# Chunks 4 to 7 score eight heads at once in two banks, and all later scores leave out the masked quarter

## The chip, the core and the metric

The kernel runs on one core of a Trainium2 chip. Its engines work from queues of their own: TensorE (PE, with its weight loads as PEld), VectorE (DVE), ScalarE (ACT), GpSimdE (POOL) and SyncE (SP, which issues most of the DMAs). The metric is the device time of one execution in microseconds (us), as the median of several runs; lower is better.

## What is computed

Three stages follow each other; the text is cut to what matters here. q, k and v have 4 batches, 8 heads, 768 positions and 64 columns a head.

```python
# retention, position by position
state = gamma * state + k[t]^T v[t]                     # 64 x 64 for each batch and head
y[t]  = 0.125 * q[t] state
x = y as 3072 tokens x 512
xn = x / sqrt(mean(x*x) + 1e-6) * rms_g                 # gated layer
x = (silu(xn @ w_gate) * (xn @ w_val)) @ w_out          # 512 -> 1536 -> 512
h = x @ w_in                                            # 512 -> 1024
solu = h * softmax(h);  ln = layernorm(solu) * g_ln
out = ln @ w_out2                                       # 1024 -> 512
```

The retention is computed in chunks of 128 positions. Within a chunk, key j and query i give a score k_j . q_i, which is multiplied by 0.125 gamma^(i-j) for i >= j and by 0 for i < j (the table `mtab`); the product, called A, is multiplied by v. What came before the chunk enters through the state U.

## The kernel before

**Blocks and chunks.** The 3072 tokens are 6 blocks of 512, and a block is 4 chunks of 128: chunks 4 to 7 belong to block 1, chunks 8 to 11 to block 2, and so on; a batch is six chunks. Block n's two layers run on PE while the chunks of block n+1 are worked on between their matmuls. So chunks 4 to 7 are computed during block 0 (from about 35 to 156 us), the others during blocks 1 to 4.

**The layers.** Each block has 12 steps m. A step is 12 matmuls for the gate into bank GB, 12 for the values into VB and 12 for the output of the step before into the four X banks; a product is three matmuls (L687 to L689: high x high, high x low, low x high), each of 512 columns in a 32-bit format. ACT makes silu from GB (L732), DVE multiplies it with VB (L704).

**The weights in block 0.** They come as 64-bit integers and are converted in 36 pieces (piece g, part 0 to 2, for step g), each some steps before PE needs it. The chain of one piece: a DMA on SP into one of four buffers `x` (L563), ACT L585, DVE L587, POOL L588, then ACT takes the signs of the piece into the PSUM bank YB (`conv_g`, L593) and DVE multiplies by them (`conv_b`, L600). ACT makes the high part (L91), DVE or POOL the low part (L92), into `w`, `wo` or `CV`, and ACT's queue stores both. In block 0 the bank YB serves the signs alone, one piece after another.

**Chunks 4 to 7 (units).** A unit is four heads of a chunk; u = 0 or 1. `unit_scores` (L159) makes four matmuls over 64 rows into bank SB, 128 x 128 each, one after another since all four lie in the same half of the rows; DVE masks them (L161). `unit_out` computes the output and the new state for the four heads, and loads what the unit after the next needs. `unit_prep` makes the decayed k and q on POOL (L143, L151).

**Chunks 8 to 23.** `att_scores` (L110 as the line of the helper) makes eight heads: the even heads lie in rows 0 to 63 and go to SB, the odd ones in rows 64 to 127 and go to YB, so two matmuls run beside each other. DVE masks bank by bank (L229). `att_out` follows some slots later; its first matmuls (SB/YB<-qd,U) are 64 x 64 and use all four quarters of the array.

**The order.** The program is written slot by slot (`slot`, `w_slot`); a scheduling layer then orders the instructions of each engine by its own model of their times, and inserts waits. Each engine runs its queue in order, so an instruction that waits holds up what is behind it.

Of the kernel before, what the change touches and what calls it, by code (L numbers as in the profile page):

```python
# [18 lines left out]
P = 128  # L19
# [21 lines left out]
def retention_moe_kernel(ctx: ExitStack, tc: tile.TileContext, qk0, q2, kt, kv, wpk, w2i, w2o,  # L41
# [38 lines left out]

    def st():
        return wt("st", [P, 512], F32, 3)
# [44 lines left out]
    def unit_load(gc, u):  # L127
        tq = wt("rq", [P, 4, P], F32, 2)
        nc.sync.dma_start(tq, q2[gc, u])
        if u == 0:  # L130
            rawk[gc] = wt("rk", [P, 4, P], F32, 2)
            nc.sync.dma_start(rawk[gc], kt[gc])
        tv = wt("rv", [P, 512], F32, 2)
        nc.sync.dma_start(tv, kv[gc, u])
        raw[gc, u] = (tq, tv)

    def unit_prep(gc, u):
        tq, tv = raw.pop((gc, u))
        tk = rawk[gc] if u == 0 else rawk.pop(gc)
        kd = qd = None  # L140
        if gc % CPB != CPB - 1:
            kd = wt("kd", [P, 4, 64], F32, 2)
            nc.gpsimd.tensor_tensor(  # L143
                out=kd, in0=tv[:, 0:256].rearrange("p (h d) -> p h d", h=4),
                in1=ktab_t[:, 4 * u:4 * u + 4].unsqueeze(2).to_broadcast([P, 4, 64]), op=ALU.mult)
        if gc % CPB != 0:
            qd = wt("qd", [P, 2, P], F32, 2)
            tq4 = tq.rearrange("p (a b) i -> p a b i", b=2)
            for hh in range(2):
                r = halfrows(hh)  # L150
                nc.gpsimd.tensor_tensor(out=qd[r], in0=tq4[r, :, hh, :],  # L151
                                        in1=qtab_t[r, 2 * u:2 * u + 2, :], op=ALU.mult)
        r = halfrows(u)
        prepd[gc, u] = (tk[r], tq[r], tv, kd, qd)
# [9 lines left out]
    def unit_out(gc, u):  # L164

        tk, tq, tv, kd, qd = prepd.pop((gc, u))
        A = masked.pop((gc, u))
        first, last = gc % CPB == 0, gc % CPB == CPB - 1
        ps = slice(2 * u, 2 * u + 2)
        calls = []  # L170
        if not first:
            calls += [mm(SB[:, pl * P:pl * P + P], U[gc % 2][:, 2 * u + pl, :], qd[:, pl, :], pl == 0, False)
                      for pl in range(2)]
        for pl in range(2):
            for hh in range(2):
                hl = 2 * pl + hh
                calls.append(mm(SB[halfrows(hh), pl * P:pl * P + P], tv[:, 256 + 64 * hl:320 + 64 * hl],
                                A[:, hl, :], first, first or pl == 1))
        sv = SB[:, 256:384].rearrange("p (a e) -> p a e", a=2)
        if not last:  # L180
            for pl in range(2):
                for hh in range(2):
                    hl = 2 * pl + hh
                    calls.append(mm(sv[halfrows(hh), pl, :], kd[:, hl, :], tv[:, 256 + 64 * hl:320 + 64 * hl],
                                    True, True))
# [12 lines left out]
    def att_load(gc):  # L198
        tq, tk = wt("rq", [P, 4, P], F32, 2), wt("rk", [P, 4, P], F32, 2)
        tv = wt("rv", [P, 2, 512], F32, 2)  # L200
# [5 lines left out]
        nc.sync.dma_start(tv, kv[gc].rearrange("u p x -> p u x"))  # L206
        raw[gc] = (tq, tk, tv)

    def att_prep(gc):
        tq, tk, tv = raw.pop(gc)  # L210
        kd = qd = None
        if gc % CPB != CPB - 1:
            kd = wt("kd", [P, 2, 4, 64], F32, 2)
# [8 lines left out]
    def att_scores(gc):  # L222
        tq, tk = prepd[gc][0:2]
        banks = (SB, YB)
        run([mm(banks[hh][:, p * P:p * P + P], tk[halfrows(hh), p, :], tq[halfrows(hh), p, :], True, True)
             for p in range(4) for hh in (1, 0)])
        for hh in (1, 0):
            A = masked[gc, hh] = wt("A", [P, 4, P], F32, 2)
            nc.vector.tensor_tensor(out=A, in0=banks[hh].rearrange("p (a i) -> p a i", a=4),  # L229
                                    in1=mtab_t[:, hh::2, :], op=ALU.mult)  # L230
# [239 lines left out]
    def att_pieces(n):  # L470

        out = []
        if n == 1:
            units = [(gc, u) for gc in range(NCB, 2 * NCB) for u in range(2)]
            ahead = units + [(2 * NCB,), (2 * NCB + 1,)]
            for i, (gc, u) in enumerate(units):
                nxt, nx2 = ahead[i + 1], ahead[i + 2]

                def a(gc=gc, u=u, nxt=nxt):
                    unit_scores(gc, u)  # L480

                def b(nxt=nxt):
                    (unit_prep if len(nxt) == 2 else att_prep)(*nxt)

                def c(gc=gc, u=u, nx2=nx2):
                    unit_out(gc, u)
                    (unit_load if len(nx2) == 2 else att_load)(*nx2)

                out += [a, b, c]
# [718 lines left out]
```

## Time and profile before

| | |
|---|---|
| runs | 993.92, 994.65 and 995.5 us, median 994.65 |
| profiled execution | 994.05 us, of which its span, first to last instruction, is 992.3 |
| PE busy | 978.1 us, 99% of the span |
| DVE, ACT, POOL busy | 453.7, 397.6 and 412.8 us |
| DMA | 211.59 MB, 213 GB/s as a mean |

Busy times overlap, since the engines run beside each other. In the timeline a row begins with its start and its duration in us, and a PE row's end is modelled: matmuls overlap, so what one costs is read from the distance between starts. One 32-bit matmul of the attention is two records. The note in brackets at a row's end is the idle time of the engine before it and who ended it.

### The profile page before, as it was taken

To read this page: it belongs to the slowest core of one execution; us is meant where nothing else is said; L and a number is where in the kernel's file an instruction comes from. 1 tells how busy PE (TensorE), PEld (TensorE's weight loads), DVE (VectorE), ACT (ScalarE), POOL (GpSimd) and SP (SyncE) were. 2 spreads that over 40 slices of the span, in tenths; PEclk is the share of its full clock that TensorE was granted. 3 is DMA by queue.
4 is the path that set the end of the run, shared out by engine and by line. 5 is a ranking of instruction groups with operands and counts; after the bars stand their busy time and mean duration, and the time that the engine had idled before them with its cause. 6 is when DMAs were issued, how large, how long until landed. Compare 5 with 4: busy or idle time off the path is not lost.

```text
span 992.3 us, 15224 instructions
## 1 busy us (share of the span) xinstructions
PE 978.1 (99%) x5654; PEld 814.7 (82%) x5654; DVE 453.7 (46%) x857; ACT 397.6 (40%) x770; POOL 412.8 (42%) x453
## 2 busy tenths in 40 slices
PE   8999999999999999999999999999999999999998
PEld 7778787888888888888888888888888888999887
DVE  5798784552453633233462223463223353443552
ACT  4767664681353452222453223334212344221433
POOL 6976883770142582252543233644032382000031
PEclk9899999999999999999999999999999999999999
DMA  9699999886412135897523889612597724687200
GB/s 353 242 329 408 351 324 347 319 321 218 164 54 86 44 125 178 292 337 262 163 75 106 287 286 311 224 49 104 174 344 266 265 79 149 216 303 257 75 8 36
DMA packets 90187, 211.59 MB, mean 213 GB/s; under 512 B 9729, under 2 KB 35713, under 8 KB 90113
## 3 DMA queue, kind: packets, MB, share of 16 engines
q1 hardware_dynamic: 81328, 185.45, 54.9%
q10 hardware_dynamic: 8784, 25.17, 6.5%
q8 instruction: 45, 0.74, 0.3%
q14 instruction: 30, 0.24, 0.1%
HBM read 171.78 MB, written 38.80 MB: 212 GB/s over the span
## 4 chain that ended last, share of the span: by engine, by line
PE 91%; POOL 3%; DMA 2%; DVE 1%; issue 1%; ACT 1%; SPq 0%; ACTq 0%; POOLq 0%
PE X L687 12%; PE X L689 12%; PE X L688 12%; PE GB L687 7%; PE GB L689 7%; PE GB L688 7%; PE VB L687 6%; PE VB L688 6%; PE VB L689 6%; PE SB L110 3%; PE YB L110 2%; PE YB L793 2%; PE VB L793 2%; PE SB L793 1%; PE GB L793 1%
## 5 line engine op out<-in xcount | busy, mean ns | idle before, releaser
L704 DVE TENSOR_TENSOR f<-VB,f 128x512 f32<-128x512 f32 x60 | 41.4, 690 | 164.0 <-PE VB L689 156.1
L688 PE MATMUL X<-r,wo 128*128 128x512 f32 x264 | 103.6, 392 | 0.0
L689 PE MATMUL X<-r,wo 128*128 128x512 f32 x264 | 103.0, 390 | 0.0
L687 PE MATMUL X<-r,wo 128*128 128x512 f32 x264 | 101.5, 396 | 0.6 <-DMA wo<-scr 0.6
L732 ACT ACTIVATE f<-GB 128x512 f32<-128x512 f32 x60 | 35.7, 595 | 153.3 <-PE GB L689 147.4
L91 ACT CAST r<-f 128x512 fp32r<-128x512 f32 x72 | 44.6, 620 | 123.6 <-DVE f L704 104.1
L588 POOL TENSOR_TENSOR st<-st,x 128x512 int32<-128x512 int32 x52 | 71.2, 1374 | 47.4 <-DVE st L587 17.0
L687 PE MATMUL GB<-xnh,w 128*128 128x512 f32 (+1 forms) x220 | 86.6, 394 | 0.8 <-ACT xnh L345 0.4
L687 PE MATMUL VB<-xnh,w 128*128 128x512 f32 (+1 forms) x220 | 85.9, 391 | 1.1 <-DVE f L704 1.1
L688 PE MATMUL GB<-xnl,w 128*128 128x512 f32 (+1 forms) x220 | 85.7, 390 | 0.5 <-DVE xnl L92 0.4
L689 PE MATMUL GB<-xnh,w 128*128 128x512 f32 (+1 forms) x220 | 85.6, 389 | 0.0
L689 PE MATMUL VB<-xnh,w 128*128 128x512 f32 (+1 forms) x220 | 85.3, 388 | 0.3 <-POOL w L92 0.3
L688 PE MATMUL VB<-xnl,w 128*128 128x512 f32 (+1 forms) x220 | 85.2, 387 | 0.0
L92 DVE TENSOR_TENSOR r<-f,r 128x512 fp32r<-128x512 f32 x72 | 62.4, 868 | 31.3 <-ACT r L91 30.8
L528 POOL TENSOR_TENSOR x<-x 128x512 f32<-128x512 f32 x24 | 31.1, 1296 | 107.3 <-DMA x<-scr 88.4
L918 POOL TENSOR_TENSOR sm<-sm 128x1 f32<-128x1 f32 x24 | 4.9, 202 | 138.6 <-DVE sm L896 116.4
L687 PEld LDWEIGHTS X<-r,wo 128*128 128x128 f32 x264 | 49.3, 188 | 11.7 <-issue 1.3
L689 PEld LDWEIGHTS X<-r,wo 128*128 128x128 f32 x264 | 49.6, 188 | 10.4
L688 PEld LDWEIGHTS X<-r,wo 128*128 128x128 f32 x264 | 49.7, 188 | 10.0 <-issue 0.2
L687 PE MATMUL X<-w2oh,r 128*128 128x512 f32 (+1 forms) x144 | 56.6, 393 | 0.0
L689 PE MATMUL X<-w2oh,r 128*128 128x512 f32 (+1 forms) x144 | 56.0, 389 | 0.0
L688 PE MATMUL X<-w2ol,r 128*128 128x512 f32 (+1 forms) x144 | 55.4, 385 | 0.0
(369 smaller groups left out, 2411.1 us busy)
## 6 DMA issues: line engine op xcount, KB each, us to landing
w<-scr SPq DMA_DIRECT2D x96, 512.0 KB, 4.8
wo<-scr SPq DMA_DIRECT2D x60, 512.0 KB, 4.5
x<-in_wpk SPq DMA_DIRECT2D x36, 512.0 KB, 6.2
x<-scr SPq DMA_DIRECT2D x24, 512.0 KB, 5.6
sscr<-x SPq DMA_DIRECT2D x24, 512.0 KB, 7.5
scr<-CV ACTq DMA_DIRECT2D x18, 512.0 KB, 6.4
rv<-in_kv SPq DMA_DIRECT2D x16, 512.0 KB, 4.2
scr<-w ACTq DMA_DIRECT2D x12, 512.0 KB, 5.3
```

What stands on the lines that cost most here:

```text
L91: h = nc.scalar.copy(hi, src)
L92: (lo_eng or nc.vector).tensor_tensor(out=lo, in0=src, in1=hi.bitcast(F32), op=ALU.subtract)
L110: return lambda: nc.tensor.matmul(out, lhsT=lhsT, rhs=rhs, start=start, stop=stop)
L528: nc.gpsimd.tensor_tensor(out=w[:, 0, :], in0=w[:, 0, :], in1=w[:, 1, :], op=ALU.add)
L588: nc.gpsimd.tensor_tensor(out=ti, in0=ti, in1=lo, op=ALU.add)
L687: nc.tensor.matmul(ps, lhsT=lh, rhs=rh, start=start, stop=False)
L688: nc.tensor.matmul(ps, lhsT=lh, rhs=rl, start=False, stop=False)
L689: nc.tensor.matmul(ps, lhsT=ll, rhs=rh, start=False, stop=stop)
L704: recent["dve"] = nc.vector.tensor_tensor(out=a, in0=GV[1], in1=silu[:, 0, :], op=ALU.mult)
L732: recent["act"] = nc.scalar.activation(s[:, 0, :], GV[0], AF.Silu)
L793: nc.tensor.matmul(ps, lhsT=x, rhs=y[:, k, :], start=start and k + i == 0, stop=k == 1 and i == 2, skip_group_check=True)
L918: G.tensor_tensor(out=w, in0=r, in1=r, op=ALU.mult)
```

## The change

For chunks 4 to 7 the units are gone. `att_load`, `att_prep` and `att_scores` serve them as they serve the later chunks, and `half_out` computes output and state for four of the eight heads at a time, in SB, with the same matmuls as `unit_out`. Since `att_scores` writes YB too, the signs of the weights (`conv_g`) and the scores use that bank in turns.

In `att_scores` each head is now two matmuls instead of one: keys 0 to 63 against all 128 queries, and keys 64 to 127 against queries 64 to 127. The quarter with late keys and early queries, where the mask is 0, is left out, and POOL sets it to 0 in A. Each matmul fills a quarter of the array (64 rows, 64 columns). For heads 4 to 7 the key halves are swapped in the output rows, so that four neighbours in the program use four different quarters; for that `att_load` loads v with its halves swapped and `turn_tables` loads the halves of `mtab` and `ktab` again the other way round. The mask is three DVE instructions a bank instead of one. `gap` only moves addresses.

```diff
-    def unit_load(gc, u):
...
-    def unit_scores(gc, u):
-        tk, tq, tv, kd, qd = prepd[gc, u]
-        for hl in range(4):
-            nc.tensor.matmul(SB[:, hl * P:hl * P + P], lhsT=tk[:, hl, :], rhs=tq[:, hl, :], start=True, stop=True)
-        A = masked[gc, u] = wt("r2", [P, 4, P], F32, 8)
-        nc.vector.tensor_tensor(out=A, in0=SB.rearrange("p (h i) -> p h i", h=4),
-                                in1=mtab_t[:, 4 * u:4 * u + 4, :], op=ALU.mult)
...
+    def half_out(gc, u):
+        tq, tk, tv, kd, qd = prepd[gc] if u == 0 else prepd.pop(gc)
+        A = [masked[gc, hh] if u == 0 else masked.pop((gc, hh)) for hh in range(2)]
...
     def att_load(gc):
...
-        nc.sync.dma_start(tv, kv[gc].rearrange("u p x -> p u x"))
+        nc.sync.dma_start(tv[:, 0], kv[gc, 0])
+        for r in range(2):
+            nc.sync.dma_start(tv[halfrows(r), 1], kv[gc, 1, halfrows(1 - r)])
+
+    def turn_tables():
+        for r in range(2):
+            nc.sync.dma_start(mtab_t[halfrows(r), 4:8, :], mtab[halfrows(1 - r), 4:8, :])
+            nc.sync.dma_start(ktab_t[halfrows(r), 4:8], ktab[halfrows(1 - r), 4:8])
...
     def att_scores(gc):
...
-        run([mm(banks[hh][:, p * P:p * P + P], tk[halfrows(hh), p, :], tq[halfrows(hh), p, :], True, True)
-             for p in range(4) for hh in (1, 0)])
+        def score(hh, p, jb):
+            half = jb if p < 2 else 1 - jb
+            return mm(banks[hh][halfrows(half), p * P + 64 * jb:p * P + P], tk[halfrows(hh), p, halfrows(jb)],
+                      tq[halfrows(hh), p, 64 * jb:P], True, True)
+
+        run([score(hh, p, jb) for jb in range(2) for a in range(2)
+             for hh, p in ((1, a), (0, 2 + a), (1, 2 + a), (0, a))])
         for hh in (1, 0):
             A = masked[gc, hh] = wt("A", [P, 4, P], F32, 2)
-            nc.vector.tensor_tensor(out=A, in0=banks[hh].rearrange("p (a i) -> p a i", a=4),
-                                    in1=mtab_t[:, hh::2, :], op=ALU.mult)
+            sc, mt = banks[hh].rearrange("p (a i) -> p a i", a=4), mtab_t[:, hh::2, :]
+            early, late = slice(0, 64), slice(64, P)
+            for ps, hs, ts_ in ((slice(0, P), slice(0, 4), late), (halfrows(0), slice(0, 2), early),
+                                (halfrows(1), slice(2, 4), early)):
+                nc.vector.tensor_tensor(out=A[ps, hs, ts_], in0=sc[ps, hs, ts_], in1=mt[ps, hs, ts_], op=ALU.mult)
+            for ps, hs in ((halfrows(0), slice(2, 4)), (halfrows(1), slice(0, 2))):
+                nc.gpsimd.memset(A[ps, hs, early], 0.0)
...
         if n == 1:
-            units = [(gc, u) for gc in range(NCB, 2 * NCB) for u in range(2)]
...
+            for gc in range(NCB, 2 * NCB):
+                out += [lambda gc=gc: att_scores(gc), lambda gc=gc: att_prep(gc + 1), lambda gc=gc: half_out(gc, 0),
+                        lambda gc=gc: (half_out(gc, 1), att_load(gc + 2))]
             return out
...
-    unit_load(NCB, 0)
-    unit_load(NCB, 1)
-    unit_prep(NCB, 0)
+    turn_tables()
+    att_load(NCB)
+    att_load(NCB + 1)
+    att_prep(NCB)
```

What the scheduling layer makes of it is shown at three places. The first is DVE's queue while PE works on step 4 of block 0. Before, a unit's mask (L161) stands between the sign products (L600, which read YB) and concerns SB only:

```order
L587 TENSOR_SCALAR st_858<-x_96_811 128x512
L600 SCALAR_TENSOR_TENSOR st_830<-st_830,YB 128x512
L161 TENSOR_TENSOR r_111_922<-SB,mtab_t 128x512
L92 TENSOR_TENSOR CV<-st_830,CV 128x512
L587 TENSOR_SCALAR st_899<-x_99_835 128x512
```

The same place in the changed kernel, where L582 is the sign product, L569 the first shift of a piece, L223 the mask and L686 the product with VB:

```order
L582 SCALAR_TENSOR_TENSOR st_810<-st_810,YB 128x512
L99 TENSOR_TENSOR r_103_939<-f_98_910,r_102_938 128x512
L99 TENSOR_TENSOR wo_886<-st_810,wo_886 128x512
L569 TENSOR_SCALAR st_891<-x_87_815 128x512
L223 TENSOR_TENSOR A_874<-YB,mtab_t 128x4x64
L223 TENSOR_TENSOR A_874<-YB,mtab_t 64x2x64 x2
L223 TENSOR_TENSOR A_880<-SB,mtab_t 128x4x64
L223 TENSOR_TENSOR A_880<-SB,mtab_t 64x2x64 x2
L582 SCALAR_TENSOR_TENSOR st_839<-st_839,YB 128x512
L569 TENSOR_SCALAR st_916<-x_92_844 128x512
```

The masks of both banks now stand between two sign products: the scores can be written only after `st_810` has used its signs, and the signs for `st_839` only after A_874 is read.

The second place is PE's queue at the end of block 0. L307 spreads the norms of block 1's tokens, from which the inputs `xnh` and `xnl` of its first matmuls are made. Before, seven matmuls of block 0 stand between it and them:

```order
L307 MATMUL SB<-ssq,ones 128x512
L689 MATMUL VB<-xnh,CV 128x512
L687 MATMUL VB<-xnh,CV 128x512
L688 MATMUL VB<-xnl,CV 128x512
L689 MATMUL VB<-xnh,CV 128x512
L689 MATMUL X_70<-r_200_1564,wo_1420 128x512
L688 MATMUL X_71<-r_201_1565,wo_1420 128x512
L689 MATMUL X_71<-r_200_1564,wo_1420 128x512
L687 MATMUL GB<-xnh,w_202_1582 128x512
L687 MATMUL VB<-xnh,w_204_1602 128x512
L688 MATMUL GB<-xnl,w_202_1582 128x512
```

In the changed kernel the same instruction is L302, and it comes after the last matmul of block 0:

```order
L670 MATMUL X_71<-r_193_1698,CV 128x512
L671 MATMUL X_71<-r_192_1697,CV 128x512
L302 MATMUL SB<-ssq,ones 128x512
L669 MATMUL GB<-xnh,w_188_1656 128x512
L669 MATMUL VB<-xnh,w_190_1676 128x512
L670 MATMUL GB<-xnl,w_188_1656 128x512
```

So no matmul is left to run between L302 and the first ones of block 1.

The third place is SP's queue before block 0. `x_31` to `x_41` are pieces of weights, `rk`, `rq` and `rv` are k, q and kv of chunk 4 and on. Before:

```order
L563 DMA x_31_438<-in_wpk 128x512
L129 DMA rq_507<-in_q 128x512
L132 DMA rk_509<-in_kt 128x512
L134 DMA rv_511<-in_kv 128x512
L129 DMA rq_513<-in_q 128x512
L134 DMA rv_515<-in_kv 128x512
L132 DMA rk_629<-in_kt 128x512
L563 DMA x_34_450<-in_wpk 128x512
L563 DMA x_37_462<-in_wpk 128x512
```

And in the changed kernel, to the same piece:

```order
L545 DMA x_31_438<-in_wpk 128x512
L179 DMA rk_513<-in_kt 64x2x128 x4
L179 DMA rq_512<-in_q 64x2x128 x4
L180 DMA rv_515<-in_kv 128x512
L182 DMA rv_515<-in_kv 64x512 x2
L179 DMA rk_528<-in_kt 64x2x128 x3
L545 DMA x_34_450<-in_wpk 128x512
L179 DMA rk_528<-in_kt 64x2x128
L179 DMA rq_527<-in_q 64x2x128 x2
L188 DMA mtab_t<-in_mtab 64x512 x2
L545 DMA x_37_462<-in_wpk 128x512
```

Ahead of `x_34` there are fourteen smaller DMAs instead of six, and five more ahead of `x_37`.

## Rows read from the trace of the kernel before

**Rows 1.** The page, part 1: busy us, share of the span, instructions.
```profile
PE 978.1 (99%) x5654; PEld 814.7 (82%) x5654; DVE 453.7 (46%) x857; ACT 397.6 (40%) x770; POOL 412.8 (42%) x453
```
**Rows 2.** PE's waits, 34 to 135 us: total us, times, longest.
```profile
PE GB L689 <- POOL CV L92: 1.2, 1, 1.2
PE SB L159 <- ACT xT L192: 0.4, 1, 0.4
```
**Rows 3.** Timeline of PE: a unit's scores in block 0.
```profile
49.47 0.61 PE L687 MATMUL X<-r,wo 128*128 128x512 f32 x2
50.01 1.16 PE L159 MATMUL SB<-rq,rk 64*128 64x128 f32 x8
...
51.44 0.39 PE L689 MATMUL X<-r,wo 128*128 128x512 f32 x1
```
**Rows 4.** Timeline of PE: the scores of eight heads, chunk 8.
```profile
256.77 0.39 PE L689 MATMUL X<-r,wo 128*128 128x512 f32 x1
257.09 0.37 PE L110 MATMUL YB<-rq,rk 64*128 64x128 f32 x1
...
258.52 0.39 PE L688 MATMUL X<-r,wo 128*128 128x512 f32 x1
```
**Rows 5.** Timeline of PE: 64 x 64 matmuls of 128 columns, chunk 8.
```profile
261.29 0.27 PE L110 MATMUL SB<-qd,U 64*64 64x128 f32 x1
...
261.31 0.27 PE L110 MATMUL YB<-qd,U 64*64 64x128 f32 x1
...
261.51 0.27 PE L110 MATMUL SB<-qd,U 64*64 64x128 f32 x1
```
**Rows 6.** Timeline of PE: matmuls of 64 columns (the state), chunk 8.
```profile
262.65 0.64 PE L110 MATMUL SB<-rv,kd 128*64 128x64 f32 x16
```
**Rows 7.** Groups by line and shape, DVE and POOL: busy us, mean ns, idle before.
```profile
L161 DVE TENSOR_TENSOR r<-SB,mtab_t 128x512 f32<-128x512 f32 x8 | 5.5, 687 | 2.6 <-PE SB L159 2.6
L279 DVE TENSOR_TENSOR U<-U,SB 128x256 f32<-128x256 f32 x11 | 4.6, 419 | 16.7 <-PE SB L110 16.7
L125 DVE TENSOR_TENSOR U<-U,SB 64x128 f32<-64x128 f32 x8 | 2.3, 282 | 0.4 <-PE SB L110 0.3
masks.py:197 POOL MEMSET ident<- 128x128 f32 x1 | 0.2, 204 | 0.3 <-POOLq L1199 0.3
```
**Rows 8.** Timeline of POOL, DVE and PE in block 0.
```profile
64.00 1.87 POOL L151 TENSOR_TENSOR qd<-rq,qtab_t 64x256 f32<-64x256 f32 x2
75.77 0.69 DVE L600 SCALAR_TENSOR_TENSOR st<-st,YB 128x512 f32<-128x512 f32 x1 [0.95 <-ACT YB L593]
79.73 1.16 PE L159 MATMUL SB<-rq,rk 64*128 64x128 f32 x8
```
**Rows 9.** Timeline of PE and DVE where block 1 begins.
```profile
154.01 1.02 PE L307 MATMUL SB<-ssq,ones 128*128 128x512 f32 x2
155.07 2.72 DVE L310 SCALAR_TENSOR_TENSOR xT<-xT,rg_t,SB 128x512 f32<-128x512 f32 x4 [4.97 <-PE SB L307]
156.81 0.50 PE L687 MATMUL GB<-xnh,w 128*128 128x512 f32 x1 [0.15 <-ACT xnh L91]
158.65 2.49 DVE L92 TENSOR_TENSOR xnl<-xT,xnh 128x512 fp32r<-128x512 f32 x4
159.39 0.50 PE L688 MATMUL GB<-xnl,w 128*128 128x512 f32 x1 [0.43 <-DVE xnl L92]
```
**Rows 10.** Timeline of SP's queue and of ACT before block 0.
```profile
15.15 0.33 SPq L129 DMA_DIRECT2D rq<-in_q  x1
...
20.94 0.43 SPq L132 DMA_DIRECT2D rk<-in_kt  x1
...
33.35 0.75 ACT L585 ACTIVATE x<-x,two 128x512 f32<-128x512 uint32 x1
```
**Rows 11.** Stretches: us; PE, PEld, DVE, ACT, POOL busy; PEclk, DMA share, GB/s.
```profile
34.70:60.00 25.30, 24.99 (x151) 20.94 (x152) 20.83 (x26) 14.56 (x24) 21.89 (x21) 0.92 0.66 220
60.00:85.00 25.00, 23.45 (x114) 18.78 (x114) 22.71 (x32) 17.94 (x32) 18.92 (x16) 1.00 1.00 374
```

More of the change, by code (lines that the diff above doesn't have):

```diff
@@ L79, in wt, with gap @@
         return wp.tile(shape, dt, tag=tag, name=f"{tag}_{cnt[0]}", bufs=bufs)
+    gaps = set()
+    def gap(name, n):
+        if name not in gaps:
+            gaps.add(name)
+            wp.tile([P, n // 4], F32, tag=name, name=name, bufs=1)
     def st():
@@ L125, in decay_add @@
             nc.vector.tensor_tensor(out=new, in0=new, in1=sv, op=ALU.add)
-    def unit_load(gc, u):
[L128 to L154, printed above, removed]
@@ L156, in unit_scores @@
-    def unit_scores(gc, u):
-        tk, tq, tv, kd, qd = prepd[gc, u]
-        for hl in range(4):
-            nc.tensor.matmul(SB[:, hl * P:hl * P + P], lhsT=tk[:, hl, :], rhs=tq[:, hl, :], start=True, stop=True)
-        A = masked[gc, u] = wt("r2", [P, 4, P], F32, 8)
-        nc.vector.tensor_tensor(out=A, in0=SB.rearrange("p (h i) -> p h i", h=4),
-                                in1=mtab_t[:, 4 * u:4 * u + 4, :], op=ALU.mult)
-    def unit_out(gc, u):
-        tk, tq, tv, kd, qd = prepd.pop((gc, u))
-        A = masked.pop((gc, u))
+    def half_out(gc, u):
+        tq, tk, tv, kd, qd = prepd[gc] if u == 0 else prepd.pop(gc)
+        A = [masked[gc, hh] if u == 0 else masked.pop((gc, hh)) for hh in range(2)]
@@ L168, in unit_out, with v @@
         first, last = gc % CPB == 0, gc % CPB == CPB - 1
         ps = slice(2 * u, 2 * u + 2)
+        def v(hl):
+            return tv[:, u, 256 + 64 * hl:320 + 64 * hl]
         calls = []
         if not first:
-            calls += [mm(SB[:, pl * P:pl * P + P], U[gc % 2][:, 2 * u + pl, :], qd[:, pl, :], pl == 0, False)
+            calls += [mm(SB[:, pl * P:pl * P + P], U[gc % 2][:, 2 * u + pl, :], qd[:, 2 * u + pl, :], pl == 0, False)
                       for pl in range(2)]
@@ L175, in unit_out @@
             for hh in range(2):
-                hl = 2 * pl + hh
-                calls.append(mm(SB[halfrows(hh), pl * P:pl * P + P], tv[:, 256 + 64 * hl:320 + 64 * hl],
-                                A[:, hl, :], first, first or pl == 1))
+                calls.append(mm(SB[halfrows(hh), pl * P:pl * P + P], v(2 * pl + hh),
+                                A[hh][:, 2 * u + pl, :], first, first or pl == 1))
         sv = SB[:, 256:384].rearrange("p (a e) -> p a e", a=2)
@@ L183, in unit_out @@
                     hl = 2 * pl + hh
-                    calls.append(mm(sv[halfrows(hh), pl, :], kd[:, hl, :], tv[:, 256 + 64 * hl:320 + 64 * hl],
-                                    True, True))
+                    calls.append(mm(sv[halfrows(hh), pl, :], kd[:, u, hl, :], v(hl), True, True))
         run(calls)
@@ L198, in att_load @@
     def att_load(gc):
+        gap("gq", 416)
         tq, tk = wt("rq", [P, 4, P], F32, 2), wt("rk", [P, 4, P], F32, 2)
+        gap("gr", 96)
         tv = wt("rv", [P, 2, 512], F32, 2)
@@ L212, in att_prep @@
         if gc % CPB != CPB - 1:
+            gap("gd", 416)
             kd = wt("kd", [P, 2, 4, 64], F32, 2)
@@ L224, in att_scores @@
         banks = (SB, YB)
[L225 to L226 removed]
+        def score(hh, p, jb):
[4 more added lines that the diff above has]
+             for hh, p in ((1, a), (0, 2 + a), (1, 2 + a), (0, a))])
         for hh in (1, 0):
+            gap("ga", 352)
             A = masked[gc, hh] = wt("A", [P, 4, P], F32, 2)
[L229 to L230 removed]
+            sc, mt = banks[hh].rearrange("p (a i) -> p a i", a=4), mtab_t[:, hh::2, :]
[5 more added lines that the diff above has]
+                nc.gpsimd.memset(A[ps, hs, early], 0.0)
     def out_calls(first, Y, Us, qd, v, A):
@@ L473, in att_pieces @@
         if n == 1:
-            units = [(gc, u) for gc in range(NCB, 2 * NCB) for u in range(2)]
[L475 to L489, printed above, removed]
+            for gc in range(NCB, 2 * NCB):
+                out += [lambda gc=gc: att_scores(gc), lambda gc=gc: att_prep(gc + 1), lambda gc=gc: half_out(gc, 0),
+                        lambda gc=gc: (half_out(gc, 1), att_load(gc + 2))]
             return out
```

## The prediction

> **What bounds the kernel now.** I read the page's busy times first. PE is busy for 978.1 of 992.3 us, every other engine for less than half [rows 1]. So the end moves by what PE has to run, and by new holes in PE's queue; work on DVE, ACT, POOL and the DMAs counts only where PE comes to wait for it. Then I read PE's waits during block 0, where this kernel differs from itself elsewhere: the two largest are 1.2 us for CV and 0.4 us for a bank that ACT had not yet read [rows 2]. Last came the timeline round the scores, and a table by stretch. That table shows where the cover is thin: from 60 to 85 us DVE is busy for 22.7 of 25.0 us and the DMA engines all the time [rows 11]. In block 0 the conversion of the weights is nearly as tight as PE.
>
> **Unit of cost.** A PE row's duration is modelled, so I take distances between starts and subtract the neighbours' pitch. A 512-column matmul costs 0.61 − 0.39 = 0.22 us, the distance between the two ends of its shape [rows 3].
>
> **Scores as they are.** A unit's four scores: from 49.47 to 51.44 are 1.97 us, in which three layer matmuls begin, so 1.97 − 3 × 0.22 = 1.31 us [rows 3]. Eight heads of a later chunk: 258.52 − 256.77 − 2 × 0.22 = 1.31 us too [rows 4]. So eight heads in two banks cost what four cost in one.
>
> **Scores as quadrants.** The trace has no matmul of 64 rows, 64 columns out and 64 streamed. The nearest is the state's product with the decayed queries: four of these, one in each quarter, with 128 columns, start within 0.02 us of each other, and the next fours follow at 0.11 us ((261.51 − 261.29)/2) [rows 5]. A pair of today's full-height scores also streams 128 columns, hence also 0.11 us, and eight pairs are 0.88 us of the 1.31. The other 0.43 us is the switch of the array's shape and the fill. The new set is four fours with 128 columns, 0.44 us, and four fours with 64. For the latter there are two ends. Below: half of 0.11, 0.055 us, if time goes with columns; the state's 64-column matmuls, on two half arrays, come out at (0.64 − 0.222)/15 = 0.028 us a record, 0.056 a pair [rows 6], the 0.222 being the mean of one. Above: 0.11 us, as with 128 columns, which is also four records at 0.028 one after another. I take the lower, since rows 5 show that four quarters start together. The set is then 0.43 + 4 × 0.11 + 4 × 0.055 = 1.09 us, or 1.31 at the upper end.
>
> The Trainium skill ("TensorEngine Tiling (Array Packing)", Instruction Overhead) says that each matmul has about 60 cycles of overhead and warns against cutting a dimension that is small already. At the full clock 60 cycles would be 25 ns, near the 28 ns a record that rows 6 show. By that rule, if the overheads of the four quarters add up, a four with 64 columns would take 0.10 us and the set about 1.27; if they lie beside each other, 1.09. Rows 5 speak for the second.
>
> **Sum of the matmuls.** Chunks 8 to 23: 16 × (1.31 − 1.09) = 3.5 us. Chunks 4 to 7: two units each before, one set now. The first unit ran before block 0, where PE waits for norms anyway, so 7 units leave and 3 sets come: 7 × 1.31 − 3 × 1.09 = 5.9 us. `half_out` issues the matmuls of `unit_out` in the same shapes: 0. Together −9.4.
>
> **Stalls in block 0.** The 1.2 us for CV follow POOL's two small products for qd, 1.87 us at 64.00 [rows 2, 8], which held a low part behind them; kd and qd are now fewer and larger instructions per chunk. The 0.4 us belongs to bank SB, which half as many score sets now claim. Both go: −1.6. What is late next? The signs share YB with the scores. In step 5's neighbourhood the sign product that must come first ended at 75.77 + 0.69 = 76.46, the scores came at 79.73 [rows 8]: 3.3 us ahead, so PE does not wait there. The next signs must wait for the scores (1.1 us) and the mask of YB (1.0 us); ACT's queue holds that conversion, and behind it the high parts and silu. The piece is then 2 to 3 us later than today, and by my estimate, from the order of the queues, still 1 to 2 us before PE wants its weights. New waits are between 0 and 4 us; I take 0.8, two stalls like the smaller of today's. Net −0.8.
>
> **Masks.** A bank's mask was 0.69 us; it becomes a 256-element instruction, about 0.42 as the state's update of that size, and two with 64 partitions and 128 elements, 0.28 each [rows 7]: 0.98. That adds 0.6 us per chunk of two banks to DVE. It is hidden by DVE's free half [rows 1]; in block 0 three chunks add 0.6 us each to stretches that have 2.3 to 4.5 us free in 25 [rows 11]. The four memsets per chunk are under 0.2 us each (128 x 128 takes 0.204) [rows 7], on POOL, before anything needs A: 0.
>
> **Start.** Up to `x_34` SP issues fourteen DMAs instead of six, up to `x_37` nineteen. At 0.33 to 0.43 us each [rows 10], thirteen more are up to 5.6 us; but the six were spread from 15.15 to 20.94 + 0.43, 6.2 us, of which their own issue is about 2.2, so 4.0 is free to take them: 0 to 1.5 us late. By the shapes 1.2 MB are ahead of `x_34` instead of 1.5 MB. I take 0, since ACT takes up the next piece only at 33.35 [rows 10]; 1.5 is the upper end.
>
> **Boundary to block 1.** L302 now has no matmul of block 0 behind it. Today L307 starts at 154.01 and the first matmul of block 1 at 156.81, but the first one that needs xnl starts at 159.39, 5.38 us after [rows 9]; in between lie the broadcast itself (0.9), nine other matmuls and a short wait: a hole of 5.38 − 0.9 − 9 × 0.22 = 2.5 us. After the change, DVE's four products (2.72 us from 155.07, i.e. +1.06 after L307) and one of the four low parts (2.49/4 = 0.62) come before the first low matmul: +4.5 counting 0.1 for the handover. PE fills it with L302 (0.9) and two matmuls (0.44): a hole of 3.2. So +0.7; bounds 0 and +2.
>
> **Sum.** The profiled execution lasted 994.05: −9.4 − 0.8 + 0.7 = −9.5, giving 984.55. It lay 0.6 below the median of the runs, 994.65, so the forecast is 985.2.
>
> **Rivals.**
> A. A four of 64 columns costs as much as one of 128. The set stays at 1.31, so 19 × 0.22 = 4.2 us are missing: 989.4. For: 0.028 a record in a row of sixteen could be a pace of issue rather than of columns [rows 6]. Against: rows 5.
> B. The conversion sets the end of block 0. If DVE and the DMAs are the bound there [rows 11], shorter PE work turns into waits for weights: the 5.9 is not seen, 991.1. For: DVE is busy for 91% and DMA for 100% of one stretch. Against: even so PE waited for only 1.6 us in all of these 100 us [rows 2], and a chunk's loads shrink from five of 256 KB to eight of 64 and 512 KB, 1.02 MB in all.
> C. The turns of YB make PE or the weights wait, 1 to 2 us for each of three sets inside block 0, beyond my 0.8: 987 to 991. For: a queue in order behind ACT's conversion. Against: 3.3 us of lead [rows 8].
> D. Slower. Two quarters over the same rows write the two halves of one bank. If these do not run beside each other, the fours go by twos: an early four takes 0.22, a late one 0.11, and the set is 0.43 + 4 × 0.22 + 4 × 0.11 = 1.75 us. Then chunks 8 to 23 lose 16 × 0.44 = 7.0, block 0 gains only 9.17 − 3 × 1.75 = 3.9, and with the stalls and the hole as above it is 994.65 + 7.0 − 3.9 − 0.8 + 0.7 = 997.7. It decides from a set of 1.59 us on, where the matmuls gain nothing: (9.17 + 16 × 1.31)/19. Against: rows 5 are the same four quarters into the same two banks, and they start together.
>
> **How the numbers follow.** Forecast 0.60, A 0.14, B 0.13, C 0.05, D 0.05, better than the range 0.03. The low end, 981, is the forecast with neither the new stalls nor the hole: −0.8 − 3.2. The high end, 991.5, takes in A, B and C, and the forecast with the start's 1.5 and a dip of the clock after the hole: from 34.7 us on, where PE had waited, the granted clock was 0.92 for 25 us [rows 11], which is 2.0 us. A measurement of this kernel tells changes from 0.2%, 2.0 us, on: 992.7 to 996.6 is no change. All cases but D lie below; parts of B with other mishaps reach into the middle: faster 0.91, same 0.04, slower 0.05.
>
> **What would show it.** In the profile after: a set in chunks 8 to 23 at 1.1 us between its neighbours less their pitch, not 1.3 (A) or 1.6 and more (D); the last chunks' blocks shorter by 0.9 us for each four chunks; PE's waits in block 0 with no CV line over 1 us and in all under 2 us (B and C would show weights, `w`, `wo` or CV, from ACT, DVE or POOL, or a wait of L117 for YB); block 1's first low matmul 4.5 us after L302; the first ACT conversion of block 0 no later than 35 us. The forecast is wrong if block 0 is not at least 5 us shorter, or if the sets of the later chunks do not shrink.

## The result: slower, 1003.3 us

The changed kernel takes 1003.27 us (median of four runs, 1002.58 to 1006.82) against 994.3: ratio 1.0083, 95% interval 1.0063 to 1.0102. The forecast was 985.2, with a range of 981 to 991.5. Its profiled execution, 1006.82 us, is the slowest of the four; before's was 994.05.

The page, part 1, after (columns as in [rows 1]):

```profile
PE 976.9 (97%) x5974; PEld 812.6 (81%) x5974; DVE 472.5 (47%) x937; ACT 400.2 (40%) x770; POOL 418.0 (42%) x521
```

PE is busy for as long as before; the span grew by 12.7 us. So I split PE's time by the starts of its rows: *wait* is the sum of the notes in brackets, *slow* what a 512-column matmul takes beyond 0.2275 us from start to start (256 columns: 0.119) where that is over 0.12 us, *work* the rest. Columns 3 to 5 run from the start of block 0 to PE's last matmul.

| profiled execution | block 0 starts | work | wait | slow |
|---|---|---|---|---|
| before | 34.7 | 947.2 | 4.3 | 2.7 |
| after | 41.5 | 936.3 | 13.9 | 9.7 |
| difference | +6.8 | −10.9 | +9.6 | +7.0 |

Not all of *slow* is the clock: 7.8 of the 9.7 us lie where the granted clock was at half (1.2 GHz), against 0.9 of the 2.7 in before; the rest is about 1.9 us in both.

The gain that the change was to bring is there. It is outweighed by three things: a late start, waits, and a slow clock behind the waits.

**The scores.** PE in chunk 8, after, and the row of before that follows its set, both for [rows 4]:

```profile
274.03 0.39 PE L671 MATMUL X<-r,wo 128*128 128x512 f32 x1
274.35 0.32 PE L117 MATMUL YB<-rq,rk 64*64 64x128 f32 x1
...
274.83 0.22 PE L117 MATMUL YB<-rq,rk 64*64 64x64 f32 x1
...
274.89 0.22 PE L117 MATMUL YB<-rq,rk 64*64 64x64 f32 x1
...
275.17 0.50 PE L669 MATMUL X<-r,wo 128*128 128x512 f32 x1
```
```profile
258.18 0.50 PE L687 MATMUL X<-r,wo 128*128 128x512 f32 x1
```

Before the set there is one matmul of the layer, behind it the next: 1.14 us from start to start. In before the same distance is 1.41 (258.18 − 256.77). So a set saves 0.26 us (0.27 by the rounded rows), and a four, that is four records in the four quarters, takes 0.06 with 64 columns (274.89 − 274.83).

**The waits**, PE, whole run (as [rows 2]):

```profile
PE X L321 <- ACT f L312: 8.2, 1, 8.2
PE GB L669 <- ACT f L714: 6.0, 5, 2.5
PE SB L293 <- ACT xT L164: 2.1, 1, 2.1
PE GB L670 <- DVE xnl L344: 1.8, 2, 1.5
PE GB L669 <- ACT xnh L98: 1.5, 1, 1.5
PE GB L670 <- DVE xnl L99: 1.2, 1, 1.2
```

The largest lies before block 0; the second is the silu, for which before hardly waited at all; the CV of [rows 2] is gone.

**The start.** PE, then ACT, then SP's queue, after:

```profile
24.58 1.14 PE L985 MATMUL SB<-f,ones 128*128 128x128 f32 x8
33.91 1.87 PE L321 MATMUL X<-ones,f 128*128 128x1 f32 x8 [8.19 <-ACT f L312]
...
41.51 0.39 PE L669 MATMUL GB<-xnh,w 128*128 128x256 f32 x1
```
```profile
25.09 0.66 ACT L98 CAST w<-st 128x512 fp32r<-128x512 f32 x1
32.33 0.34 ACTq L615 DMA_DIRECT2D scr<-w  x1
32.72 0.66 ACT L575 ACTIVATE sq<-x 128x512 f32<-128x512 f32 x1 [6.96 <-DMA x<-in_wpk]
```
```profile
14.65 5.79 SPq L179 DMA_DIRECT2D rk<-in_kt  x4
20.48 3.74 SPq L179 DMA_DIRECT2D rq<-in_q  x4
...
28.09 0.51 SPq L545 DMA_DIRECT2D x<-in_wpk  x1
```

ACT stands still from 25.8 to 32.3, in front of the store of a weight, and the squares (L312) for the norms are behind it. In the program each DMA waits for the one eight DMAs ahead of it in the planned order. For this store that is now the load of `x_34`, which lands 4.2 us after its issue, at 32.3; in before it was the first q load, which had landed at 23.6, 1.1 us before the store went out. `x_34` is issued at 28.1 instead of 21.7. In both kernels the first four loads behind `x_31` go out only as their turn of eight comes, up to about 20 us. Behind them before has two, at 0.43 us each, and after has ten, most at 0.5 to 0.7 us and one at 1.6. The issue of the k and q loads among the fourteen, after (x, then ns: least, median, most):

```profile
L179 SPq DMA_DIRECT2D rk<-in_kt x7: 534/596/659, 14.7 to 27.4; - x7
L179 SPq DMA_DIRECT2D rq<-in_q x4: 534/602/1631, 20.5 to 23.7; - x4
```

**A wait for the silu**, ACT's queue in step 8, after; L714 is the silu, L164 and L167 are chunk 6's output and its square, the others convert weights:

```profile
127.10 0.62 ACT L98 CAST CV<-st 128x512 fp32r<-128x512 f32 x1 [1.34 <-DVE st L582]
127.62 0.62 ACT L575 ACTIVATE YB<-x 128x512 f32<-128x512 f32 x1
128.63 0.78 ACT L567 ACTIVATE x<-x,two 128x512 f32<-128x512 uint32 x1 [0.39 <-DMA x<-in_wpk]
130.06 0.62 ACT L98 CAST CV<-st 128x512 fp32r<-128x512 f32 x1 [0.65 <-DVE st L582]
...
130.64 0.37 ACT L164 COPY xT<-SB 128x256 f32<-128x256 f32 x1
130.91 0.64 ACT L575 ACTIVATE YB<-x 128x512 f32<-128x512 f32 x1
131.46 0.62 ACT L167 ACTIVATE f<-xT 128x512 f32<-128x512 f32 x1
131.98 0.59 ACT L714 ACTIVATE f<-GB 128x512 f32<-128x512 f32 x1
```

GB was complete at 124; the silu came 8 us later, and PE waited for 2.1. In the order of ACT's queue a silu of block 0 comes 10 to 19 rows behind the one before it in before, 7 to 27 after: 26 in step 5 and 27 in step 8, where the scores have held YB and the conversions pile up behind them (run 4 tests this).

**The slow clock**, PE behind the first wait for a silu, after, and two stretches, the slow one and what follows (columns as [rows 11]):

```profile
53.46 0.50 PE L669 MATMUL GB<-xnh,CV 128*128 128x512 f32 x1 [2.49 <-ACT f L714]
...
55.02 0.63 PE L669 MATMUL GB<-xnh,CV 128*128 128x512 f32 x1
55.45 0.63 PE L670 MATMUL GB<-xnl,CV 128*128 128x512 f32 x1
...
58.59 0.39 PE L669 MATMUL VB<-xnh,CV 128*128 128x512 f32 x1
58.82 0.40 PE L670 MATMUL VB<-xnl,CV 128*128 128x512 f32 x1
```
```profile
55.00:58.00 3.00, 3.00 (x8) 2.34 (x7) 3.00 (x4) 2.08 (x5) 2.81 (x2) 0.50 0.65 210
58.50:75.00 16.50, 16.50 (x94) 13.40 (x93) 14.32 (x23) 11.62 (x21) 11.88 (x11) 1.00 0.93 308
```

The pitch is 0.43 us from 55.0 to 58.0 (1.2 GHz) and 0.23 afterwards (2.4 GHz): 1.5 us on top of a wait of 2.49. The same follows the wait at 132.6 and those at the boundary (175.3 and 177.2), 1.5 us each; behind the wait at 162.7 the stretch is twice as long and costs 3.1. In before only the start has such a stretch, up to 38.8 us; at its boundary the granted clock is 1.00:

```profile
150.00:165.00 15.00, 13.28 (x55) 9.84 (x54) 7.46 (x13) 6.87 (x12) 7.79 (x5) 1.00 0.90 348
```

**The boundary**, PE, after (as [rows 9]):

```profile
172.77 1.02 PE L302 MATMUL SB<-ssq,ones 128*128 128x512 f32 x2
175.28 0.50 PE L669 MATMUL GB<-xnh,w 128*128 128x512 f32 x1 [1.49 <-ACT xnh L98]
...
177.21 0.50 PE L670 MATMUL GB<-xnl,w 128*128 128x512 f32 x1 [1.19 <-DVE xnl L99]
```

### The profile page after: what moved, and what is told of

It is laid out like the page before. It is cut to its first block, busy times and chain, and to the rows that moved or that the text cites. A ratio compares the mean times of both kernels' runs of the same rounds, so it can differ in the third digit from the quotient of the medians.

```text
span 1005.0 us, 16133 instructions
## 1 busy us (share of the span) xinstructions
PE 976.9 (97%) x5974; PEld 812.6 (81%) x5974; DVE 472.5 (47%) x937; ACT 400.2 (40%) x770; POOL 418.0 (42%) x521
## 4 chain that ended last, share of the span: by engine, by line
PE 79%; DMA 2%; POOL 1%; SPq 1%; DVE 1%; issue 1%; ACT 0%; ACTq 0%; POOLq 0%
PE X L669 11%; PE X L671 11%; PE X L670 11%; PE GB L669 6%; PE GB L671 6%; PE GB L670 6%; PE VB L669 5%; PE VB L670 5%; PE VB L671 5%; PE SB L117 2%; PE YB L117 2%; PE VB L775 2%; PE YB L775 2%; PE GB L775 1%; PE SB L775 1%; DMA x<-in_w2i 1%
## 5 line engine op out<-in xcount | busy, mean ns | idle before, releaser
L686 DVE TENSOR_TENSOR f<-VB,f 128x512 f32<-128x512 f32 x60 | 41.3, 688 | 161.6 <-PE VB L671 147.6
L714 ACT ACTIVATE f<-GB 128x512 f32<-128x512 f32 x60 | 35.7, 595 | 154.7 <-PE GB L671 151.4
L99 DVE TENSOR_TENSOR r<-f,r 128x512 fp32r<-128x512 f32 x72 | 64.6, 899 | 29.7 <-ACT r L98 28.9
```

Of the source, the lines that this page charges most:

```text
L99: (lo_eng or nc.vector).tensor_tensor(out=lo, in0=src, in1=hi.bitcast(F32), op=ALU.subtract)
L686: recent["dve"] = nc.vector.tensor_tensor(out=a, in0=GV[1], in1=silu[:, 0, :], op=ALU.mult)
L714: recent["act"] = nc.scalar.activation(s[:, 0, :], GV[0], AF.Silu)
```

## The experiments

Verdicts go by the medians; the kernel before ran beside each on the same chip. Part of every edit is that the scheduling layer orders the queues anew.

**1. Three loads a chunk.**

```diff
-                    nc.sync.dma_start(t[halfrows(hh), 2 * u:2 * u + 2, :], heads[:, :, hh, :])
-        nc.sync.dma_start(tv[:, 0], kv[gc, 0])
...
+        nc.sync.dma_start(tk, kt[gc])
+        nc.sync.dma_start(tq, q2[gc])
+        nc.sync.dma_start(tv, kv2[gc].rearrange("u p x -> p u x"))
```

> The changed kernel, with q, k and kv of a chunk laid out in memory in the order in which the tiles hold them, so that att_load issues three DMAs of 256, 256 and 512 KB instead of eleven, and turn_tables two instead of four; nothing else is edited. Theory L (the loads: their issue on SP and their 512-byte packets hold up the pieces of the weights, which are behind them in SP's queue) expects the start of block 0 back from 41.5 to 34 to 36 us, no wait of PE over 1.5 us in block 0, and 983 to 989 us. Theory Y (the turns of signs and scores in bank YB hold up ACT and through it PE) expects only the start to come back: 995 to 998, with the waits for silu in block 0 as they are. Theory M (the longer masks on DVE and the memsets on POOL) expects the same as Y.

993.72 us; to before 0.9994 (0.9984 to 1.0004). The start is back but for 1.5 us (36.2), wait 9.8, slow 6.0, work 938.0. The loads were worth 9.5 us. Theory L expected more, 983 to 989 and no wait over 1.5 us; instead 9 us of waits and slow time more than in before take the place of the gain, with one wait of 2.7 us for a silu.

**2. Three loads for chunks 4 and 5 alone.**

```diff
+        if gc < NCB + 2:
+            nc.sync.dma_start(tk, kp[gc - NCB])
+            nc.sync.dma_start(tq, qp[gc - NCB])
+            nc.sync.dma_start(tv, kv2[gc - NCB].rearrange("u p x -> p u x"))
+            return
```

> The changed kernel with three loads for chunks 4 and 5 alone, the two that are loaded before block 0; chunks 6 to 23 keep their eleven, and the tables their four. In the planned order each DMA waits for the one eight DMAs ahead of it. For ACT's first store of a weight that is, in the changed kernel, the load of x_34, which SP issues only at 28.1 us behind fourteen small loads; ACT stands still from 25.8 to 32.3 us, and the norms and PE with it. Here it is the kv load of chunk 4. If that is the start's 6.9 us, block 0 starts at 35 to 38 us and the time falls from 1003.3 to 996 to 999; the rest of the 9.5 us that three loads gave everywhere belongs to the loads inside block 0. If the late start had to do with the bytes or the turned tables instead, it stays at 40 us and more.

995.82 us; to before 1.0013 (1.0003 to 1.0023). Block 0 starts at 34.5. ACT at the same place:

```profile
25.60 0.34 ACTq L620 DMA_DIRECT2D scr<-w  x1
26.00 0.67 ACT L580 ACTIVATE sq<-x 128x512 f32<-128x512 f32 x1 [0.23 <-ACT w L98]
```

The store is issued at 25.6 instead of 32.3. These two chunks' loads, 22 of the change's, are 7.4 of the 9 us that it lost. The turned tables, still loaded in four parts, are not the cause. That the way leads through ACT's store is what the order and these rows show. Wait and slow stay at 11.1 and 6.3: they take the place of the shorter work (937.2).

**3. Small loads in the kernel before.**

```diff
-        nc.sync.dma_start(tq, q2[gc, u])
...
+        for hh in range(2):
+            nc.sync.dma_start(tq4[:, :, hh, :], heads[:, :, hh, :])
```

(k in four parts, the second kv in two.)

> The kernel before, with the loads of a unit cut into eleven DMAs a chunk instead of five, of 64 to 256 KB, with the same bytes and 512-byte packets for q and k; scores, masks and banks as before. Theory L expects it to be slower by 8 to 18 us: 1002 to 1012. Theories Y and M expect no more than 3 us: 994 to 997.

996.95 us, 1.0019 (1.0006 to 1.0033): block 0 starts 3.7 us later, and wait is 2.9 and slow 2.2, no more than without. The late start is there; theory L's stalls inside block 0 are not, and its 8 to 18 us are missed by far.

**4. Signs in SBUF**, with the eleven loads:

```diff
-        g = YB if begun[0] else wt("sq", [P, 512], F32, 1)
+        g = wt("sq", [P, 512], F32, 1)
```

> The changed kernel, with the signs of the weights written to the SBUF tile sq in block 0 too, as before block 0, so that YB serves the scores alone. Theory Y expects block 0 to lose most of its 12 us of waits: 990 to 995. Theory L expects little: 1000 to 1005, with the start at 41 to 42 us.

1008.74 us, slower still: `sq` also serves the later chunks' squares, and block 1 gets 5.7 us of new waits. So the edit was made again for block 0's weights alone (`if begun[0] and not isinstance(key[0], int)`), with three loads and with eleven.

> The kernel with three loads a chunk, with the signs of block 0's weights in the SBUF tile sq (those of the second layer's weights, from block 1 on, stay in YB). Between two silus ACT's queue then has 10 to 20 instructions, as in the kernel before (10 to 19), instead of 9 to 26. Theory Y2 (the turns of YB pile the conversions up in ACT's queue, ahead of a silu that PE needs) expects no wait for silu over 0.5 us in block 0, waits from its start to chunk 8 at 2 to 5 us instead of 8.7, and 984 to 989 us. Theory B (the conversion as such is the pace of block 0, wherever the signs lie) expects the waits to come back under other names: 992 to 995.

> The changed kernel with its eleven loads, and the signs of block 0's weights in sq in the same way. With the run above, the one with three loads and the changed kernel it makes a table of two by two. If loads and turns add up, this one lies as far below the changed kernel (1003.3) as the run above lies below the one with three loads (993.7): 993 to 998, with the start still at 41 to 42 us. Theory B: 1001 to 1004.

994.59 (0.9980 to 1.0012) and 1003.19 us. From silu to silu ACT's queue has 10 to 20 rows again, 7 to 18 in the second, and in the first PE waits for no silu in block 0 at all (in the second for two, 3.0 us); yet its wait and slow are 10.0 and 4.0, the waits now for `r`, `w`, CV. Theory Y2's time is missed: the waits came back under other names. But the edit is not free, as the table behind run 7 shows.

**5. No quadrants**: eight heads at once for chunks 4 to 7, one full-height matmul a head, one mask a bank, nine loads.

```diff
-        run([score(hh, p, jb) for jb in range(2) for a in range(2)
-             for hh, p in ((1, a), (0, 2 + a), (1, 2 + a), (0, a))])
+        run([mm(banks[hh][:, p * P:p * P + P], tk[halfrows(hh), p, :], tq[halfrows(hh), p, :], True, True)
+             for p in range(4) for hh in (1, 0)])
```

> The changed kernel without quadrants: chunks 4 to 7 take eight heads at once, in turns with the signs, but every score is one matmul of full height, the mask one instruction a bank, no memsets, no turned tables; nine loads a chunk instead of eleven. Theory L expects that it stays slower than the kernel before: 19 sets cost 0.26 us more each than in the changed kernel (5 us), the loads a little less: 1000 to 1008. Theory M expects the masks' share back: 995 or less plus the 5 us of the sets, so 996 to 1000.

1003.68 us (1.0064 to 1.0126): as slow as the whole change, with block 0 starting at 39.5. So the first part of the change, not the quadrants, brought the loss; and theory M, which blamed the masks and memsets (996 to 1000), is missed.

**6. Quadrants alone**: before's units in chunks 4 to 7, quadrants and three loads from chunk 8 on, the tables turned after the last unit.

> The kernel before with its units, loads and banks in chunks 4 to 7 untouched, and quadrants for chunks 8 to 23 alone; their q, k and kv are laid out in memory as the tiles hold them (three loads a chunk), and the tables' halves are turned after the last unit. All theories expect block 0 as before (start 34 to 36, start to chunk 8 221 to 224) and 16 sets at 0.26 us less: 989 to 991. If the quadrants cost something that the sets do not show (masks, memsets, loads), it stays at 993 to 996.

994.76 us, 0.9995 (0.9984 to 1.0005): a miss. From chunk 8's scores to the end 3.9 us are gained, as expected; the profiled run, the slowest of its ten, has lost them in a start 2.1 us later and 3.7 us more of wait and slow in block 0. Part of that start may be chance: PE waited for the first kv load, 2.2 us against 1.6 in before. Where the medians lose the gain is not shown.

**7. An earlier tail**, on experiment 1:

```diff
-                begin, span, r = 0, 30, (31, 32, 33, 33, 33, 33, 34, 34, 35, 35)
+                begin, span, r = 0, 27, (29, 30, 31, 31, 32, 32, 33, 33, 34, 34)
```

> The kernel with three loads a chunk, with the pieces of chunks 4 to 7 spread over 27 slots of block 0 instead of 30 and the steps of block 1's norms two slots and one slot earlier. Theory T expects the broadcast (161.2 us) to come without a wait and the holes round it to shrink by 2 to 5 us: 987 to 991. Theory B expects the waits to move elsewhere: 992 to 996.

997.31 us (1.0014 to 1.0036). Inconclusive: the split of block 1's inputs now comes before step 11's products in program order, which then read block 1's inputs in place of their own, so PE waits for 5.9 us there. With 28 slots and `r` untouched, on experiment 4:

> The first of these three with the pieces of chunks 4 to 7 spread over 28 slots of block 0 instead of 30 (the steps of block 1's norms stay where they are), so that the broadcast of the norms stands in front of step 11's matmuls, which fill the time until block 1's inputs are ready. If the hole at the boundary is what is left, its 2 to 4 us go: 981 to 987, below the first of these runs by 2 or more.

994.23 us (0.9971 to 1.0000). PE no longer waits for block 1's inputs, and 1.7 us for its norms instead; wait and slow are 8.2 and 4.2: still no clear gain.

**What paces block 0?** All repaired versions stop at 994. The lead of a weight (from the end of its low part to the start of the first matmul of its step; gate and value, steps 4 to 10, median and extremes) tells; beside it stands DVE's busy time from 36 to 150 us, 114 us in all:

| | lead, us | DVE, us | run, us |
|---|---|---|---|
| before | 3.9 (1.7 to 6.4) | 93.5 | 994.3 |
| after | 2.6 (0.2 to 5.3) | 94.7 | 1003.3 |
| three loads | 0.7 (−1.5 to 2.7) | 96.0 | 993.7 |
| and signs in SBUF | 0.6 (−3.4 to 4.0) | 104.2 | 994.6 |
| and 28 slots | 1.6 (−1.3 to 5.9) | 105.5 | 994.2 |

(It can be below 0: the first product of a step takes the high part alone.) PE has caught up with the conversion. The jump of DVE's time comes with the signs in SBUF. Their product, the same instruction in the same shape, with three loads and with 28 slots (36 to 150 us, columns as [rows 7]):

```profile
L576 DVE SCALAR_TENSOR_TENSOR st<-st,YB 128x512 f32<-128x512 f32 x29 | 19.8, 682 | 4.3 <-ACT YB L569 4.0
L576 DVE SCALAR_TENSOR_TENSOR st<-st,sq 128x512 f32<-128x512 f32 x30 | 32.9, 1096 | 1.0 <-ACT sq L569 1.0
```

With the signs in the PSUM bank each takes 0.67 to 0.69 us, with the signs in SBUF 0.67 to 1.79. So the repair of run 4 loads DVE with some 8 us more, and what is tried below on the version with 28 slots is tried with a dearer product than the changed kernel has.

**8. Without signs** (ACT has less to do, DVE as much):

```diff
-        nc.scalar.activation(g, half[key][1], AF.Sign, scale=2.0 ** -135)
-        half[key].append(g)
+        half[key].append(half[key][0])
```

> The kernel with three loads a chunk, and without the signs of the weights: conv_g does nothing and conv_b takes a minimum and a maximum of the tile with itself, so the weights of block 0 lose their signs, ACT has 0.6 us a piece less to do, and YB serves the scores alone. Theory B (the conversion of the weights paces block 0, so PE's shorter work there became waits) expects PE's waits between the start of block 0 and chunk 8 to fall from 8.7 to under 4 us, and 981 to 987 us. Theory T (block 1's norms come late, since chunk 7's output is copied late in ACT's queue; no pace of the conversion) expects the waits at the end of block 0 as they are: 989 to 993.

> The kernel before, without the signs of the weights in the same way. PE waited for 3.6 us in its block 0, so theories B and T both expect a gain of 0 to 4 us: 990 to 995. It is the measure for the run without signs: what that one gains beyond this one is what the conversion cost the changed kernel.

1000.76 and 1012.57 us: less work, and both slower. The longest new waits lie in block 1, 3.3 us for a silu and 4.5 for DVE's product. Why the new order brings them is not shown; no reading of the pace can rest on these two.

**9. Half the stores, or neither signs nor the product with them**, both on the version with 28 slots, and each on before:

```diff
-        stores.append((scr[g][part], w.bitcast(F32)))
+        stores.append((scr[g][part][:, 0], w.bitcast(F32)[:, 0]))
```
```diff
     def conv_b(key):
-            lastc[0] = nc.vector.scalar_tensor_tensor(out=t, in0=t, scalar=3.4028234663852886e38, in1=g,
-                                                      op0=ALU.min, op1=ALU.mult)
...
+        done64[key] = half.pop(key)[0]
```

> The kernel with three loads, signs in SBUF and 28 slots, with only the high half of each piece of the weights stored in block 0 (256 KB instead of 512) and read back for both halves later, so from block 1 on the low parts of the weights are the high parts; all else as it was. In the kernels with three loads the lead of a piece (from its low part being written to its first matmul) has sunk from 2 to 6 us in steps 4 to 10 to about 0: the weights now pace block 0. Theory D (by the DMAs, which are busy for 95 to 100% there) expects the leads back at 2 us and more, PE's waits in block 0 from 5.6 to under 3 us, and 984 to 990 us. Theory V (by the chain of conversion on DVE and POOL) expects no change: 992 to 995.

> The kernel before with the same half stores, as the measure: there the leads are 2 to 6 us and PE waits for 3.6 us in block 0, so theory D expects at most 2 us (992 to 995), theory V nothing (994 to 995).

> The kernel with three loads, signs in SBUF and 28 slots, without the signs and the product with them: conv_g and conv_b do nothing, the weights of block 0 lose their signs and their upper bound, ACT has 0.6 us and DVE 0.7 us a piece less; the DMAs are untouched. Theory V expects leads of 2 us and more and 983 to 989 us; theory D leads near 0 and 991 to 995.

> The kernel before without the signs and the product with them, as the measure for the 983.3 us of the changed one without it. Before has 3.6 us of waits and 2.3 us of slow clock in block 0 and leads of 2 to 6 us, so theory V expects a gain of 0 to 5 us (989 to 995), and the changed kernel 6 to 11 us below it, which is what PE's shorter work is worth.

Half stores: 1012.56 and 1007.41 us. Without the product: 983.25 (0.9860 to 0.9889) and 989.56 (0.9941 to 0.9970). The same stretch with 28 slots as it was, with half stores, and without the product:

```profile
85.00:110.00 25.00, 25.00 (x165) 19.59 (x164) 23.71 (x31) 16.26 (x30) 20.79 (x19) 1.00 0.96 330
```
```profile
85.00:110.00 25.00, 19.61 (x111) 14.88 (x110) 21.69 (x30) 15.64 (x28) 19.80 (x17) 0.91 0.81 270
```
```profile
85.00:110.00 25.00, 25.00 (x188) 19.95 (x187) 15.12 (x28) 12.45 (x22) 19.53 (x22) 1.00 0.96 345
```

Half stores took the DMAs from 0.96 to 0.81, and the leads rose to 12 us (7.7 on before), as theory D had it, so theory D's pace is not refuted. Yet the time rose, by 18 and 12 us, against both theories: PE waited more, for masks and outputs behind conversions in DVE's and ACT's queues.

Without the product DVE is busy for 15.1 of 25 us instead of 23.7, the leads are 4.3 us (1.2 to 7.8), wait and slow fall from 8.2 and 4.2 to 5.5 and 1.3, with the DMAs as full as ever: leads and time lie where theory V expected them. Of the 11 us, 4.5 are an earlier start of block 0 (31.7 instead of 36.2); before gains as much there (30.5 instead of 34.7). So the measure is the difference of the two kernels: 989.56 − 983.25 = 6.3 us, or 8 us if each is taken by its ratio to the kernel before beside it, is what the repaired change is worth with a lighter conversion. With the full one it is at most 3 us (run 7, 0.9971 to 1.0000). So the work of the conversion holds the gain back; through which engine is not shown, since the cut takes work from DVE and from ACT. Run 8 took the signs alone and gained nothing.

**10. One mask a bank**, with the same result, since the table is 0 in the quarter that no matmul writes:

```diff
-                nc.vector.tensor_tensor(out=A[ps, hs, ts_], in0=sc[ps, hs, ts_], in1=mt[ps, hs, ts_], op=ALU.mult)
...
-                nc.gpsimd.memset(A[ps, hs, early], 0.0)
+            nc.vector.tensor_tensor(out=A, in0=banks[hh].rearrange("p (a i) -> p a i", a=4),
+                                    in1=mtab_t[:, hh::2, :], op=ALU.mult)
```

> The kernel with three loads, signs in SBUF and 28 slots, with one mask instruction a bank instead of three and no memsets: the quarter that no matmul writes holds what the bank held before, and the table's 0 turns it to 0. DVE has about 0.5 us and POOL 1 us a chunk less to do. Theory V (the work of DVE and POOL paces block 0) expects a gain of 1 to 3 us over 994.2, so 991 to 993; theory D none.

> The same single mask in the kernel with three loads, signs in SBUF and the pieces over 30 slots (994.6). Theory V: 991 to 994; theory D: 994 to 995.

With 28 slots 991.02 us, 0.9959 (0.9944 to 0.9975): faster than both kernels, with three loads, signs in SBUF and quadrants. With 30 slots 993.94 (0.9982 to 1.0001), within noise. The gain lies in theory V's range, but its way is not seen: DVE is as busy as without the edit (105.3 of 114 us), and the leads are the same (1.6). In the profiled execution block 0 starts 1.6 us earlier and *slow* is 2.0 less; why is not shown.

## Why the prediction was wrong

1. **The matmuls: right.** Forecast −9.4, measured −10.9 of work. A four of 64 columns costs about half of one with 128, as taken from rows 5; a set saves 0.26 us instead of 0.22. Rivals A and D did not occur. The Trainium skill ("TensorEngine Tiling (Array Packing)", Instruction Overhead) gives each matmul an overhead of about 60 cycles, so that one with a single column takes as long as one with 60. The trace does not show these overheads adding up over the four quarters: fours of 64 columns start 0.06 us apart, not the 0.10 that the prediction worked out for that case.
2. **Start, "I take 0", with 1.5 as the upper end: failed, +6.8.** I priced fourteen loads, most of them small, by the issue of six large ones [rows 10] and asked only when the piece is needed by its own conversion. The nearer price stood in the trace of before, where the later chunks load in the same form:

```profile
134.32 2.57 SPq L205 DMA_DIRECT2D rk<-in_kt  x4
```

   That is 0.64 us each. And the turn of eight, by which a late load holds ACT's store and the norms behind it, was not followed past SP. Run 2 shows this step alone to be 7.4 us.
3. **"Stalls in block 0 … Net −0.8": failed, +8.0, and 6.9 more of slow clock behind them and the boundary.** (The other 1.6 of the +9.6 lie at the boundary and later.) The old stalls went as forecast. That PE would not wait for the scores was right as well (3.3 us of lead); I wrote that ACT's queue holds "behind it the high parts and silu" and then counted only the weights' time, not the silu's. No term stood for the slow clock behind such a wait; the trace shows 1.5 us on top of the waits at 53.5 and 132.6, and 3.1 behind the one at 162.7.
4. **Rival B, at 0.13, comes nearest to the rest**: the conversion takes the gain of block 0, 991.1. With the loads repaired the time is 994, the leads have sunk to 0.6 to 1.6 us, and run 9 shows that a lighter conversion frees 6 to 8 us. B's reason, DVE and the DMAs at their bound, is not shown for the changed kernel: DVE is hardly busier there than before (94.7 and 93.5 of 114 us), and only the repair with signs in SBUF makes it so. Nor did PE wait for weights as B had it, but mostly for silu and norms. "DVE's free half" of [rows 1], which was to hide the masks, is a mean over blocks that convert nothing; what the masks cost in block 0 is not shown, since run 10 gained without making DVE less busy.
5. **Boundary: right in size** (4.4 us from L302 to the first low matmul, forecast 4.5), and the slow clock behind the hole came too, 1.5 us, which stood only in the high end of the range.

Open: how much of the waits in each version is the new order alone. Runs 6 and 8 suggest several us, and no run here holds the order fixed. Open too is which engine paces the conversion: fewer DMAs and less work on DVE and ACT both lengthened the leads.

## What to carry to other kernels

Where PE's inputs are made beside it, a shorter PE gains only what they lie ahead: first look how far that is, and whose work sets it. Count DMAs, not bytes, and follow each added one to every queue that takes a turn behind it, stores of other engines included. Price a PE wait with the slow stretch that may follow it. And measure what a repair itself adds before building on it, as with the signs in SBUF.

## What the runs showed of the hardware

In the changed kernel each of PE's three waits of 2.1 to 2.5 us from 53 to 163 us was followed, 0.7 to 1.4 us after PE resumed, by 3.4 us (twice) or 6.8 us at a granted clock of half (1.2 GHz), 0.43 us a matmul instead of 0.23. In the two kernels of experiment 4 with signs in SBUF for block 0, waits of 2.1 and 2.5 us passed without one, and in the first kernel of experiment 7 one of 3.4 us; what tells them apart was not tried. Four records of 64 x 64 in the four quarters start every 0.06 us with 64 columns, every 0.11 with 128. Loads of 64 KB in 512-byte rows took SP 0.53 to 0.66 us each to issue at the start, and one 1.6, where 256 KB loads of the kernel before took 0.33 to 0.43. DVE's product of two 128 x 512 tiles took 0.67 to 0.69 us with one of them in PSUM, and 0.67 to 1.79 with both in SBUF.
